# A chunked attention and its MLP on one core: the order written out by hand, attention of the next 384 tokens between the steps of the MLP

## The chip, the cores and the metric

The kernel runs on one core of one Trainium2 chip. A core has five engines with a queue of instructions each: TensorE (PE, with its weight loads shown apart as PEld) multiplies matrices and transposes, VectorE (DVE), ScalarE (ACT) and GpSimd (POOL) work on tiles, and SyncE (SP) issues transfers. Matrix products land in PSUM, an accumulator memory of eight banks; everything else lies in SBUF. Transfers from and to memory are issued from POOL's or SP's queue and run on 16 DMA engines. The metric is the time on the device in microseconds (us), lower is better.

## What is computed

Two stages in a row, over 4 batches of 768 tokens. Inputs and output are float32.

```python
def _attn_ref(q, k, v, mem_k, mem_v):          # q, k, v: (4, 8, 768, 64); mem: 8 rows per head
    chunk, left_ctx, right_ctx = (32, 16, 8)
    for c in range(nc):                        # 24 chunks of 32 tokens
        l_start = max(0, c_start - left_ctx)
        r_end = min(S, c_end + right_ctx)
        k_full = np.concatenate([mem_k, k[:, :, l_start:r_end]], axis=2)
        v_full = np.concatenate([mem_v, v[:, :, l_start:r_end]], axis=2)
        scores = scale * np.matmul(q_c, k_full.transpose(0, 1, 3, 2))
        a = np.exp(scores - max)
        out[:, :, c_start:c_end] = np.matmul(a / sum(a), v_full)

def _moe_ref(x, g_ln, w_ch1, w_ch2):           # x: (4, 768, 512), the heads side by side
    xn = (x - mu) / np.sqrt(var + 1e-06) * g_ln
    return x + np.maximum(xn @ w_ch1, 0.0) @ w_ch2      # 512 -> 2048 -> 512
```

Each chunk of 32 queries sees at most 56 keys around it and 8 memory keys. The second stage is a layer normalisation and an MLP with a residual.

## The kernel before

The kernel works batch by batch and has seven segments, each a function. All matrices are held in float16, cast by the transfers that load them.

`load_kq` and `load_v` (issued from POOL, L98, L102, L111, L116, L120) bring k, q and v of a batch; tokens stand on the partitions in blocks of 128, so a transfer consists of rows of 64 elements. `v16` holds, for each of eight groups of 96 queries, the 120 value rows around it (neighbouring groups overlap) behind 8 memory rows that `bcast_mem_v` copies (L130), and a column of ones that gives the sum of the softmax.

`seg_B(b)` transposes k and q with TensorE, head by head (L188, L193 for the memory keys, L210), into a PSUM tile `trp` of 64 partitions; DVE copies k into `slabs` in four pieces (L198, L199, L203, L204), so that each group of 96 queries has its own 128 keys beside the memory keys, and q into `QT` (L215).

`seg_C(b)` computes, for each group and half of the heads, four products of 128 keys by 96 queries (L222), and ACT takes the exponential in three pieces with a bias `bandcol` that puts keys outside a chunk's band at -50 (L231).

`seg_D(b)` multiplies the weights with the values (L253) in blocks of 32, 64 or 96 rows, divides by the sum (L261, L264), and normalises: statistics on DVE (L270, L271), the square root on ACT (L272), reciprocal and shift on DVE (L276, L277), and the application on ACT (L282).

`seg_E(b)` transposes the normalised rows (L292) and ACT copies them out (L297). `seg_F(b, pi)` is the up projection of 384 tokens: 16 PSUM tiles of 128 x 384, four matmuls each (L305), and the ReLU on DVE (L311). `seg_G(b, pi)` is the down projection: three PSUM tiles of 128 x 512, sixteen matmuls each (L320), the residual on DVE (L327) and the store from SP (L328).

PSUM is shared as four banks `trp`, two `mm` (scores, values and the up projection take turns there) and two `f2p`. The code asks for the segments in the order F, C, G, F, D, G, B, E for each batch (L341 to L354), but the order in which each engine gets its instructions is set by a scheduler that may move any instruction forward past others that do not depend on it. In the trace, for example, the scores of the next batch run between down matmuls, and single down matmuls between up groups.

The weights come by `load_w1` and `load_w2` (L134, L141); `scale_w1` multiplies the layer norm's gain into `w1s` (L178). In the order of POOL's queue they stand behind k, q and v of the first batches.

## Time and profile before

| | us |
|---|---|
| median of 3 runs | 315.42 |
| lowest and highest run | 315.36, 317.46 |
| profiled execution, span from the first to the last instruction | 317.2 |

| engine | busy us in the profiled execution |
|---|---|
| PE | 275.5 |
| PEld | 158.7 |
| DVE | 183.2 |
| ACT | 102.0 |
| POOL | 71.9 |

A busy time adds up the stretches in which an engine has at least one instruction under way. Matmuls overlap each other, so a busy TensorE need not be a TensorE at its peak: the distance from one start to the next says how dense it is. The chain of waits follows the last instruction back to what released each step. A group of instructions is given with its line, its engine, output and inputs by the program's names, shapes, count, busy time and the mean duration of one; behind the bar stands how long the engine had been idle before them and what ended that. In a timeline, instructions of one kind that follow one another are merged, with their count.

### The profile page before, as it was taken

Reading aid. Unit: us, or ns where it says so; the run is one execution under the profiler, and the core shown is the slowest. Engines: PE = TensorE matmul, PEld = TensorE weight load, DVE = VectorE, ACT = ScalarE, POOL = GpSimd, SP = SyncE. Lnnn points to the kernel's source line nnn. Section 1 sums busy time; section 2 is a strip of 40 time slices with the busy share of each in tenths; the row PEclk is TensorE's granted clock in tenths of the full one; section 3 lists DMA queues with packets and bytes.
Section 4 is the critical chain, followed back from the end, with each engine's and each line's share of the span. In section 5 each row is a group of like instructions: output and inputs, shape, how many; then the busy total and the mean of one; then the engine's idle time right before and its main releaser. Section 6 shows DMA issues by size and latency. Waiting matters only on the chain.

```text
span 317.2 us, 5313 instructions
## 1 busy us (share of the span) xinstructions
PE 275.5 (87%) x2112; PEld 158.7 (50%) x2112; DVE 183.2 (58%) x519; ACT 102.0 (32%) x264; POOL 71.9 (23%) x88
## 2 busy tenths in 40 slices
PE   0794776497999999799999999789999995999994
PEld 0673655363534555475434554655435543455441
DVE  3571369953614787956506788957117784577411
ACT  0026734330287014330494034230990145100000
POOL 8977052993000020900000012800000000000000
PEclk9999999997999999969999999799999999799999
DMA  8999999999991021950011031910010010000121
GB/s 51 155 124 140 194 151 144 86 130 200 160 87 68 1 18 66 108 36 2 0 67 36 0 51 39 127 10 2 33 36 33 2 66 35 0 0 2 55 77 66
DMA packets 90695, 21.11 MB, mean 67 GB/s; under 512 B 85040, under 2 KB 87088, under 8 KB 90672
## 3 DMA queue, kind: packets, MB, share of 16 engines
q0 software_dynamic: 86688, 14.50, 63.0%
q1 hardware_dynamic: 3984, 6.30, 5.4%
q8 instruction: 16, 0.26, 0.4%
q14 instruction: 7, 0.06, 0.1%
HBM read 28.97 MB, written 6.29 MB: 111 GB/s over the span
## 4 chain that ended last, share of the span: by engine, by line
PE 76%; DVE 8%; DMA 5%; ACT 5%; POOL 3%; issue 2%; ACTq 0%; POOLq 0%; DVEq 0%
PE f2p L320 28%; PE mm L305 26%; PE mm L222 6%; PE mm L253 5%; PE trp L210 5%; PE trp L188 4%; DMA w2s<-in_moe_w_ch_dram 3%; ACT AT L231 3%; DMA q<-in_q_dram 2%; DVE bnst L270 2%; ACT xnT L297 1%; DVE x L264 1%; DVE w1s L178 1%; POOL v L111 1%; PE trp L193 1%
## 5 line engine op out<-in xcount | busy, mean ns | idle before, releaser
L320 PE MATMUL f2p<-w2s,reluT 128*128 128x512 f16 x384 | 106.5, 382 | 2.2 <-DMA w2s<-in_moe_w_ch_dram 2.2
L305 PE MATMUL mm<-xnT,w1s 128*128 128x384 f16 x512 | 99.4, 332 | 3.8 <-ACT xnT L297 2.7
L311 DVE TENSOR_SCALAR reluT<-mm 128x384 f16<-128x384 f32 x128 | 71.0, 557 | 46.1 <-PE mm L305 41.1
L305 PEld LDWEIGHTS <-w1s 128*128 128x128 f16 x512 | 49.8, 99 | 44.5 <-issue 11.1
L231 ACT ACTIVATE AT<-mm,bandcol 128x128 f16<-128x128 f32 x192 | 53.9, 369 | 9.0 <-PE mm L222 6.7
L320 PEld LDWEIGHTS <-reluT 128*128 128x128 f16 x384 | 31.2, 97 | 28.7 <-issue 0.2
L327 DVE TENSOR_TENSOR out_sb<-f2p,x 128x512 f32<-128x512 f32 x24 | 16.5, 686 | 45.0 <-PE f2p L320 45.0
L188 PE MATMUL trp<-identity,k 128*64 128x128 f16 x192 | 25.9, 282 | 17.7 <-DMA k<-in_k_dram 9.1
L111 POOL DMA_DIRECT2D v<-in_v_dram x32 | 27.5, 866 | 28.2 <-PE mm L253 26.4
L116 POOL DMA_DIRECT2D v<-in_v_dram x8 | 6.6, 819 | 103.6 <-PE mm L253 103.5
L188 PEld LDWEIGHTS <-k 128*64 128x64 f16 x192 | 18.7, 147 | 22.3 <-issue 12.1
L253 PEld LDWEIGHTS <-AT 128*64 128x64 f16 (+2 forms) x448 | 20.1, 115 | 19.4 <-issue 14.8
L253 PE MATMUL mm<-v,AT 128*64 128x65 f16 (+2 forms) x448 | 25.4, 212 | 4.9 <-DVE x L264 4.9
L222 PE MATMUL mm<-QT,slab 64*128 64x96 f16 x256 | 24.1, 221 | 5.6 <-ACT AT L231 5.6
L222 PEld LDWEIGHTS <-slab 64*128 64x128 f16 x256 | 14.5, 102 | 27.8 <-issue 27.8
L282 ACT ACTIVATE xn<-x,negmr,rstd 128x512 f16<-128x512 f32 x24 | 19.5, 813 | 23.7 <-DVE negmr L277 23.7
L231 ACT ACT_TABLE_LOAD x4 | 5.1, 1283 | 60.3 <-DVE reluT L311 39.8
L210 PE MATMUL trp<-identity,q 128*64 128x128 f16 x192 | 23.8, 280 | 0.7 <-DMA q<-in_q_dram 0.7
L199 DVE COPY slab<-trp 64x720 f16<-64x720 f16 x32 | 16.4, 514 | 8.8 <-PE mm L222 8.7
L272 ACT ACT_TABLE_LOAD x4 | 5.1, 1283 | 47.5 <-DVE recip L261 47.4
L264 DVE TENSOR_TENSOR x<-mm,recip 128x256 f32<-128x256 f32 x48 | 19.7, 411 | 0.4
L215 DVE COPY QT<-trp 64x768 f16<-64x768 f16 x32 | 17.2, 538 | 2.0 <-PE trp L210 1.8
(36 smaller groups left out, 166.0 us busy)
## 6 DMA issues: line engine op xcount, KB each, us to landing
out_dram<-out_sb SPq DMA_DIRECT2D x24, 256.0 KB, 2.0
k<-in_k_dram POOLq DMA_DIRECT2D x8, 384.0 KB, 8.4
q<-in_q_dram POOLq DMA_DIRECT2D x8, 384.0 KB, 8.9
v<-in_v_dram POOLq DMA_DIRECT2D x32, 90.0 KB, 4.7
w1s<-in_moe_w_ch_dram POOLq DMA_DIRECT2D x4, 512.0 KB, 13.7
w2s<-in_moe_w_ch_dram POOLq DMA_DIRECT2D x4, 512.0 KB, 11.9
v<-in_v_dram POOLq DMA_DIRECT2D x16, 60.0 KB, 4.2
mem_k<-in_mem_k_dram POOLq DMA_DIRECT2D x1, 32.0 KB, 2.8
```

Of the source, the lines that this page charges most:

```text
L111: nc.gpsimd.dma_start(out=v16[hh][8:128, hp, 1:7, 0:64], in_=dram_ap(v, base + hp * S * D + 80 * 64, [[64, 120], [96 * 64, 6], [1, 64]]),)
L188: nc.tensor.matmul(out=ktr[:, 128 * i : 128 * i + 128], lhsT=k16[b % 2][:, h, i, :], rhs=identity, is_transpose=True, start=(i == 0), stop ...
L210: nc.tensor.matmul(out=qtr[:, 128 * i : 128 * i + 128], lhsT=q16[b % 2][:, h, i, :], rhs=identity, is_transpose=True, start=(i == 0), stop ...
L215: nc.vector.tensor_copy(out=QT[hh][:, hp, :], in_=qtr)
L222: nc.tensor.matmul(out=sc[:, QG * hp : QG * hp + QG], lhsT=slabs[4 * hh + hp][:, g, :], rhs=QT[hh][:, hp, QG * g : QG * g + QG], start=(hp ...
L231: nc.scalar.activation(out=atv[:, :, 32 * t : 32 * t + 32], in_=scv[:, :, 32 * t : 32 * t + 32], func=mybir.ActivationFunctionType.Exp, bi ...
L253: nc.tensor.matmul(out=av[r0:r1, hp, :], lhsT=ATt[g][hh][:, QG * hp + ql : QG * hp + ql + (r1 - r0)], rhs=v16[hh][:, hp, g, :], start=(hp ...
L264: nc.vector.tensor_tensor(out=xs[t][b % 2][:, 256 * hh : 256 * hh + 256], in0=av[:, :, 0:64], in1=rc_b, op=mybir.AluOpType.mult,)
L282: nc.scalar.activation(out=xn16[t], in_=xt, func=mybir.ActivationFunctionType.Identity, bias=negmr[j], scale=rstd[j],)
L305: nc.tensor.matmul(out=o, lhsT=w1s[dt][:, 128 * hc : 128 * hc + 128], rhs=xnT[dt][:, 384 * pi : 384 * pi + 384], start=(dt == 0), stop=(dt ...
L311: nc.vector.tensor_scalar(out=reluT[pi][hc], in0=o, scalar1=0.0, scalar2=None, op0=mybir.AluOpType.max,)
L320: nc.tensor.matmul(out=o2, lhsT=reluT[pi][hc][:, 128 * (t % 3) : 128 * (t % 3) + 128], rhs=w2s[hc // 4][:, hc % 4, :], start=(hc == 0), st ...
```

## The change

The kernel is written anew around units of 384 tokens, and the scheduler is switched off: each engine runs its instructions in the order in which the code asks for them. While the MLP of unit u runs, the attention of unit u+1 is put between its steps.

A unit has 28 steps: 16 up steps (four matmuls of 384 columns and a ReLU) and 12 down steps (four matmuls of 512 columns, the residual and the store after each fourth). The attention of 128 tokens is a call of `scores`, one of `values` and one of `turn_x`; three of each follow steps 1, 5, 10, then 8, 12, 17, then 15, 19, 24. In units 0, 2 and 4 the next batch's keys and queries are transposed by four calls of `kq_block` after steps 3, 7, 11 and 17. The loads of a batch to come stand at step 20 of units 0 and 2 (`load_kq`) and at steps 2 to 5 of units 1 and 3 (`load_v` and what belongs to it).

Shapes change as well:

- k and q lie with 8 tokens of a head on a partition (96 partitions), so a transfer has rows of 512 elements. `kq_block` transposes two heads of k and q, 32 transposes of 96 columns, to the two halves of 128 partitions. DVE copies k and ACT copies q out, each as 768 elements on 128 partitions. `KT` holds the keys in blocks of 72 columns, 64 tokens and 8 memory keys, so that a group of 64 queries finds all its keys in 104 neighbouring rows and no keys are copied twice.
- `scores` takes groups of 64 queries: eight matmuls of 64 columns and 64 rows per group, alternating between the two row halves and between two PSUM banks, and two exponentials of 256 elements on 104 partitions, with the band as a bias.
- `values`: sixteen matmuls of 65 columns, alternating between the two groups, whose outputs lie on the two halves of the partitions. The division is one instruction of 512 elements instead of two of 256.
- The normalisation: statistics on DVE as before; the shift, the sum with 1e-6, its power of -1/2 and the application to the row (512 elements) are four instructions on POOL. ACT has no part in it.
- The ReLU goes to ACT in odd up steps and stays on DVE in even ones.
- The value rows of neighbouring groups are copied on the chip (`load_v_halo`, `load_v_mem`, from SP) instead of being loaded twice.
- The weights lie in chunks by output column, `w1c`, `w2c`, and are loaded, in the order of POOL's queue, w1 behind k and q of batch 0 and the first 7 of its 12 value blocks, then the other 5 blocks, then w2, and k, q and v of batch 1 behind all of these.
- PSUM: `att` has two tiles of two banks each, `f1p` two of one bank (up), `f2p` two of one bank (down).

The core of the diff, the new code:

```diff
+    ctx.enter_context(tc.manual_schedule())
+    att = [ps.tile([128, 2, 512], FP32, name=f"att{i}") for i in range(2)]
+    f1p = [ps.tile([128, 384], FP32, name=f"f1p{i}") for i in range(2)]
+    f2p = [ps.tile([128, 512], FP32, name=f"f2p{i}") for i in range(2)]
...
+    def load_kq(b):
+        for dst, src in ((k16, k), (q16, q)):
+            nc.gpsimd.dma_start(
+                out=dst[b % 2][:, :, :, :],
+                in_=dram(src, b * H * HS, [[512, 96], [HS, H], [1, 512]]),
+            )
+    def load_v(b, g0, g1):
+        vt = V[b % 2]
+        for g in range(g0, g1):
+            nc.gpsimd.dma_start(
+                out=vt[24:88, g, :, 0:64],
+                in_=dram(v, b * H * HS + 64 * g * D, [[64, 64], [HS, H], [1, 64]]),
+            )
...
+    def mem_cols(b):
+        src = memKT[:, 4 * b : 4 * b + 4, :]
+        nc.gpsimd.tensor_copy(
+            out=free(KT[b % 2], 16, [[KC, 4], [BLK, NG + 1], [1, 8]]),
...
+    def kq_block(b, j):
+        p = slot("att")
+        for half, src in ((0, k16), (1, q16)):
+            pv = as16(p[:, half, :])
+            for r in range(8):
+                for par in range(2):
+                    nc.tensor.matmul(
+                        out=pv[64 * par : 64 * par + 64, 96 * r : 96 * r + 96],
+                        lhsT=src[b % 2][:, 2 * j + par, r, :], rhs=identity[0:96, 0:96],
+                        is_transpose=True, start=True, stop=True,
+                        tile_position=(0, 64 * par),
+                    )
+        pk, pq = as16(p[:, 0, :]), as16(p[:, 1, :])
+        nc.vector.tensor_copy(
+            out=free(KT[b % 2], j * KC + 24, [[BLK, NG], [8, 8], [1, 8]]),
+            in_=free(pk, 0, [[8, NG], [1, 8], [96, 8]]),
+        )
+        nc.scalar.copy(
+            out=free(QT[b % 2], j * S, [[8, 96], [1, 8]]),
+            in_=free(pq, 0, [[1, 96], [96, 8]]),
+        )
+    def scores(b, t):
+        for g in (2 * t, 2 * t + 1):
+            p = slot("att")
+            a = AT[g % 4]
+            for j in range(4):
+                for par in range(2):
+                    nc.tensor.matmul(
+                        out=p[:, par, 64 * j : 64 * j + 64],
+                        lhsT=KT[b % 2][64 * par : 64 * par + 64, j, BLK * g : BLK * g + 128],
+                        rhs=QT[b % 2][64 * par : 64 * par + 64, j, 64 * g : 64 * g + 64],
+                        start=(j == 0), stop=(j == 3), tile_position=(64 * par, 0),
+                    )
+            for c in range(2):
+                nc.scalar.activation(
+                    out=free(a, 32 * c, [[64, 2], [128, 4], [1, 32]], KR),
+                    in_=free(p, 32 * c, [[512, 2], [64, 4], [1, 32]], KR),
+                    func=ACTF.Exp, bias=band[0:KR, cls, c : c + 1], scale=0.125,
+                )
+    def values(b, t, x):
...
+        for h in range(H):
+            for gg in range(2):
+                nc.tensor.matmul(
+                    out=p[64 * gg : 64 * gg + 64, h // 4, c0 : c0 + HD],
+                    lhsT=AT[g % 4][0:KR, h, :], rhs=V[b % 2][0:KR, g, h, :],
+                    start=(h % 4 == 0), stop=(h % 4 == 3), tile_position=(0, 64 * gg),
+                )
...
+        nc.vector.bn_stats(out=bst[i], in_=x)
+        nc.vector.bn_aggr(out=mv[i], in_=bst[i])
+        nc.gpsimd.tensor_scalar(out=lnc[i][:, 0:1], in0=mv[i][:, 0:1], scalar1=-1.0, scalar2=1.0, op0=ALU.mult, op1=ALU.mult)
+        nc.gpsimd.tensor_scalar(out=lnc[i][:, 1:2], in0=mv[i][:, 1:2], scalar1=1e-6, scalar2=1.0, op0=ALU.add, op1=ALU.mult)
+        nc.gpsimd.tensor_tensor(out=lnc[i][:, 2:3], in0=lnc[i][:, 1:2], in1=mhalf[:, 0:1], op=ALU.pow)
+        nc.gpsimd.tensor_scalar(
+            out=xn[i], in0=x, scalar1=lnc[i][:, 0:1], scalar2=lnc[i][:, 2:3],
+            op0=ALU.add, op1=ALU.mult,
+        )
...
+        if hc % 2:
+            nc.scalar.activation(out=rT[u % 2][hc], in_=p, func=ACTF.Relu)
+        else:
+            nc.vector.tensor_scalar(
+                out=rT[u % 2][hc], in0=p, scalar1=0.0, scalar2=None, op0=ALU.max
+            )
...
+    nc.gpsimd.dma_start(out=memk16, in_=dram(mem_k, 0, [[64, 8], [512, B * H], [1, 64]]))
+    load_kq(0)
+    nc.gpsimd.dma_start(out=memv16[:, :, :, 0:64], in_=dram(mem_v, 0, [[64, 8], [512, B * H], [1, 64]]))
+    load_v(0, 0, 7)
+    make_identity(nc, identity)
+    load_w1(0)
...
+    mem_keys()
+    mem_cols(0)
+    load_w1(1)
+    load_w1(2)
+    load_w1(3)
+    load_v(0, 7, NG)
+    for c in range(4):
+        load_w2(c)
+    mem_cols(1)
...
+    for j in range(4):
+        kq_block(0, j)
+    scores(0, 0)
+    scores(0, 1)
+    values(0, 0, xs[0])
+    scores(0, 2)
+    values(0, 1, xs[1])
+    turn_x(0, 0)
+    values(0, 2, xs[2])
+    turn_x(0, 1)
+    for c in range(4):
+        scale_w1(c)
+    turn_x(0, 2)
+    load_kq(1)
+    load_v_halo(0, 6, NG)
+    load_v(1, 0, NG)
...
+    for u in range(NU):
+        b1, half = (u + 1) // 2, (u + 1) % 2
...
+        if u + 1 < NU:
+            for i in range(3):
+                t = 3 * half + i
+                at(1 + 7 * i, scores, b1, t)
+                at(5 + 7 * i, values, b1, t, xs[(3 * (u + 1) + i) % 9])
+                at(10 + 7 * i, turn_x, u + 1, i)
+        if u % 2 == 0 and u // 2 + 1 < B:
+            bn = u // 2 + 1
+            for j in range(4):
+                at((3, 7, 11, 17)[j], kq_block, bn, j)
+            if bn + 1 < B:
+                at(20, load_kq, bn + 1)
+        if u % 2 == 1 and u // 2 + 2 < B:
+            bn = u // 2 + 2
+            at(2, load_v, bn, 0, NG)
+            at(3, mem_cols, bn)
...
+        for step in range(28):
+            if step < 16:
+                up(u, step)
+            else:
+                down(u, (step - 16) // 4, (step - 16) % 4)
+            for fn, args in plan.get(step, ()):
+                fn(*args)
```

More of the change, by code (lines that the diff above doesn't have):

```diff
@@ L45 @@
     identity = sb.tile([128, 128], FP16, name="identity")
[L46 to L47 removed]
+    memk16 = sb.tile([8, B * H, 64], FP16, name="memk16")
+    memv16 = sb.tile([8, B, H, HD], FP16, name="memv16")
+    memKT = sb.tile([128, B * 4, 8], FP16, name="memKT")
     g_col = sb.tile([128, 4], FP32, name="g_col")
[L49 to L50 removed]
@@ new lines, in as16 @@
+    def as16(t):
+        return t.bitcast(FP16)
+    HS = S * D
+    def load_kq(b):
[11 more added lines that the diff above has]
+            )
```

472 lines of the change are left out of this document (180 added, 292 removed).

## The prediction

> **What bounds the kernel now.** I read the page first (span, busy time, chain), then busy time by stretches, then TensorE's timeline.
>
> ```profile
> span 317.2 us, 5313 instructions
> PE 275.5 (87%) x2112; PEld 158.7 (50%) x2112; DVE 183.2 (58%) x519; ACT 102.0 (32%) x264; POOL 71.9 (23%) x88
> GB/s 51 155 124 140 194 151 144 86 130 200 160 87 68 1 18 66 108 36 2 0 67 36 0 51 39 127 10 2 33 36 33 2 66 35 0 0 2 55 77 66
> PE 76%; DVE 8%; DMA 5%; ACT 5%; POOL 3%; issue 2%; ACTq 0%; POOLq 0%; DVEq 0%
> HBM read 28.97 MB, written 6.29 MB: 111 GB/s over the span
> q0 software_dynamic: 86688, 14.50, 63.0%
> ```
>
> By stretches (columns: stretch, busy time and instructions of each engine, granted TensorE clock, DMA share, GB/s written):
>
> ```profile
> core 0: us, PE busy (x) PEld busy (x) DVE busy (x) ACT busy (x) POOL busy (x), PEclk, DMA share, GB/s
> 9.00:25.00 16.00, 14.78 (x114) 11.71 (x115) 11.06 (x41) 2.53 (x6) 14.19 (x24) 1.00 2.77 134
> 25.00:42.00 17.00, 11.63 (x102) 9.04 (x102) 2.93 (x11) 13.47 (x46) 4.87 (x7) 1.00 1.85 181
> 143.00:212.00 69.00, 65.57 (x527) 36.19 (x527) 45.00 (x130) 25.47 (x66) 10.24 (x12) 0.98 0.30 38
> ```
>
> TensorE ends the chain, but 87% is an average of two unlike parts. From 143 to 212 us, one batch of the steady loop, TensorE is idle for 3.4 us; from 25 to 42 us it is idle for 5.4 while the loads run at their highest. How dense the loop is shows only in start-to-start distances, in TensorE's timeline (start, length, operation):
>
> ```profile
> 74.54 0.38 PE L320 MATMUL f2p<-w2s,reluT 128*128 128x512 f16 x1 [2.22 <-DMA w2s<-in_moe_w_ch_dram]
> 74.75 2.21 PE L305 MATMUL mm<-xnT,w1s 128*128 128x384 f16 x8
> 76.76 0.63 PE L320 MATMUL f2p<-w2s,reluT 128*128 128x512 f16 x1
> 77.19 2.22 PE L305 MATMUL mm<-xnT,w1s 128*128 128x384 f16 x8
> 79.25 0.38 PE L320 MATMUL f2p<-w2s,reluT 128*128 128x512 f16 x1
> ...
> 86.43 0.34 PE L222 MATMUL mm<-QT,slab 64*128 64x96 f16 x4
> 86.70 1.90 PE L320 MATMUL f2p<-w2s,reluT 128*128 128x512 f16 x8
> 88.54 0.34 PE L222 MATMUL mm<-QT,slab 64*128 64x96 f16 x4
> ...
> 106.67 1.46 PE L305 MATMUL mm<-xnT,w1s 128*128 128x384 f16 x8
> 107.97 0.38 PE L320 MATMUL f2p<-w2s,reluT 128*128 128x512 f16 x1
> ...
> 116.78 0.33 PE L253 MATMUL mm<-v,AT 128*64 128x65 f16 x8
> 117.04 1.04 PE L320 MATMUL f2p<-w2s,reluT 128*128 128x512 f16 x4
> ...
> 128.85 0.52 PE L210 MATMUL trp<-identity,q 128*64 128x128 f16 x6
> 129.21 0.50 PE L188 MATMUL trp<-identity,k 128*64 128x128 f16 x6
> ```
>
> and, from the chain of waits, its last stretch of TensorE and a group of exponentials:
>
> ```profile
> 36.59 1.67 ACT AT L231 x6
> ...
> 295.37 17.71 PE f2p L320 x82
> ```
>
> Eight 384-column matmuls take 106.67 to 107.97: 0.1625 us each. The last 82 of 512 columns take 17.71: 0.216. The MLP is 512 x 0.1625 + 384 x 0.216 = 166.1 us before and after. A 128-column transpose in a warm stream takes (129.21 - 128.85)/6 = 0.06 us, a 65-column value matmul (117.04 - 116.78)/8 = 0.0325, the shortest spacing here. Eight down matmuls between score groups take 88.54 - 86.70 = 1.84 instead of 1.73, and the four scores 0.27 instead of 4 x 0.0425 (96 columns at the 384-column rate): about 0.1 on entry, 0.1 on exit, 0.2 per excursion.
>
> So of 317.2 us, 166 are MLP matmuls, some 70 are a start that waits for loads (at 74.54 the first down matmul still waits for `w2s`), 4.1 are the tail (313.08 to the end), and the rest is attention inside three loop rounds of 69 us.
>
> **The change, part by part.** Other prices, from the groups (last numbers: busy time, mean ns of one, idle before), then three rows of the timeline:
>
> ```profile
> L231 ACT ACTIVATE AT<-mm,bandcol 128x128 f16<-128x128 f32 x192 | 53.9, 369 | 9.0 <-PE mm L222 6.7
> L297 ACT ACTIVATE xnT<-trp 128x768 f16<-128x768 f16 x16 | 12.0, 810 | 18.1 <-PE trp L292 13.2 <-DVE slab L204 4.8
> L311 DVE TENSOR_SCALAR reluT<-mm 128x384 f16<-128x384 f32 x128 | 71.0, 557 | 46.1 <-PE mm L305 41.1
> L327 DVE TENSOR_TENSOR out_sb<-f2p,x 128x512 f32<-128x512 f32 x24 | 16.5, 686 | 45.0 <-PE f2p L320 45.0
> L270 DVE BATCH_NORM_STATS2 bnst<-x 128x6 f32<-128x512 f32 x24 | 16.4, 683 | 0.0
> L261 DVE RECIPROCAL recip<-mm 128x4 f32<-128x4 f32 x48 | 8.1, 169 | 7.7 <-PE mm L253 7.4
> L215 DVE COPY QT<-trp 64x768 f16<-64x768 f16 x32 | 17.2, 538 | 2.0 <-PE trp L210 1.8
> L155 POOL TENSOR_SCALAR_AFFINE_SELECT bandcol<-zcol 128x3 f32<-128x3 f32 x2 | 0.4, 194 | 0.0
> masks.py:199 POOL TENSOR_SCALAR_AFFINE_SELECT identity<-identity 128x128 f16<-128x128 f16 x1 | 0.3, 304 | 0.1
> L120 POOL DMA_DIRECT2D v<-in_v_dram x8 | 6.3, 790 | 0.0
> ```
>
> ```profile
> 3.22 1.44 POOL L98 DMA_DIRECT2D k<-in_k_dram  x1
> 9.07 0.85 PE L188 MATMUL trp<-identity,k 128*64 128x128 f16 x6 [9.07 <-DMA k<-in_k_dram]
> 17.87 2.50 POOL L111 DMA_DIRECT2D v<-in_v_dram  x3 [1.78 <-DMA q<-in_q_dram]
> ```
>
> *TensorE in the loop.* A unit is 384 tokens: 16 up steps of 4 x 0.1625 = 0.65 and 12 down steps of 4 x 0.216 = 0.866, 20.8 us. Beside it stand, three times, scores (16 matmuls), values (16) and `turn_x` (4 transposes, 0.23). Values: 16 x 0.0325 + 0.2 = 0.72. Scores have 64 columns and load 128-column weights; no row shows a pair on two row halves, so their spacing lies between 0.0145 (two at once at the 64-column rate of 0.029) and 0.0425 (the 96-column one); I take 0.0325, the nearest measured small matmul: 0.72. `kq_block`: 32 transposes of 96 columns, alternating between column halves: between 0.021 (pairs at once) and 0.0425 (one by one); I take the middle, 0.032, so 1.22 with the excursion. A unit with the next one's attention is 20.8 + 3 x (0.72 + 0.72 + 0.23) = 25.8; units 0, 2 and 4 carry four `kq_block`s more: 30.7; unit 7 is 20.8.
>
> *DVE and ACT.* The page's busy times (183 and 102) would not bind, but the order is now fixed, and `f1p` has two buffers: up step n waits for the ReLU of step n-2. After values(5) DVE does reciprocal 0.17, multiply 0.69, statistics 0.68, aggregate 0.17 = 1.71, and only then ReLU 6 (0.557). By hand, from a unit's start: values end at 5.42, DVE's chain at 7.26, ReLU 6 at 7.82; TensorE is ready for up 8 at 6.72 and starts at 7.85: 1.1 lost. After scores(8), four exponentials of 256 elements hold ACT: 0.369 + 128 x 0.69 ns (the slope from the 768-element copy, 0.81) = 0.46 alone; six of 128 take 1.67, 0.28 apart, 0.09 less than one lasts, so four take some 1.5; ReLU 9 follows and up 11 waits 0.2. Elsewhere results are early. An odd unit is 27.2 us. In an even one the `kq_block` at step 7 covers the 1.1; with its own copies (768 scattered elements on DVE, between 0.54 as the packed `QT` copy and 0.94 at the 1 ns per element between L311 and L327; I take 0.94) I find 0.3: 31.0. Bounds: no stall to 3 us per unit.
>
> *Normalisation moves from ACT to POOL*: three one-column instructions (about 0.2 each, as the 3-element select) and one over 512 elements: 0.19 + 0.45 by the slope between the two selects, up to 0.9 for its two operations; 1.5 together. In an odd unit DVE's chains end at 7.3, 14.8 and 21.95, and TensorE comes to `turn_x` at 10.5, 17.4 and 24.4: 3.2, 2.6 and 2.45 us. Covered, so nothing; if the cover goes, each microsecond is paid per tile. ACT's switches between exponential and square root go too, none on TensorE's path.
>
> *POOL's queue.* The tile scheduler before hid the load issues; now `load_v` (12 issues of 0.8) stands before the unit's normalisation. At 17.87 the fourteenth POOL transfer waits for the sixth, the second `q`: eight are in flight at most. In unit 0 (31.0 long) values(19) end at 23.9, DVE at 25.8, POOL at 27.3; it then issues `load_kq(2)`, six `v`, and stops until k and q (3.15 MB) have landed, then five more issues and `mem_cols`. q lands at 27.3 + 3 (before bytes flow) + 3.15/0.362 = 39.0; five issues (4.0), `mem_cols` (0.7, as a select) and the normalisation (1.5) make 45.2, which is 14.2 of unit 1, whose `turn_x` is due at 10.5: 3.7 lost, and likewise in unit 3: 7 us (0 to 10).
>
> *The start.* Loads run at 181 GB/s written between 25 and 42 us; q0 writes 14.5 MB for 28.97 read, so 362 GB/s read. Until `kq_block(1, 0)` at step 3 of unit 0 the queue carries kq(0) 3.15, v(0) 1.57, w1 and w2 8.39, kq(1) 3.15 = 16.25 MB, one behind the other; before, v(1) and kq(2) also stood ahead of w2. The first 0.79 MB landed 5.8 us after its issue (3.22 to 9.07), 3.6 more than its bytes; with `k` issued at 2.2 by a shorter instruction the flow starts at 5.2, 16.25/0.362 = 44.9 later it is 50, and I add 3 for gaps: the identity now stands behind seven `v` issues and thus behind q's landing (about 14), the weights behind it and behind twelve selects. q(1) lands at 53 (bounds: 46 at 400 GB/s, twice the 200 of the page's fastest slice, 66 at the 268 that 134 written in 9:25 gives). The MLP itself can start earlier: from an identity at 15.5, 128 transposes of 0.05 to 0.1 and three tiles of scores, values and normalisation (some 5 each) end at 38 to 44. TensorE then reaches step 3 and waits, so the landing decides.
>
> *The sum*, in the profiled execution's time: landing 53; rest of unit 0 from the q half of that block, 31.0 - 3.9 = 27.1; TensorE's slow first steps after a wait, 1.5 (the eight after 74.75 and the eight after 77.19 take 2.0 each for 1.3); units 1, 3, 5, 6: 4 x 27.2 = 108.8; units 2 and 4: 62.0; unit 7: 20.8; POOL 7; tail 4.1: 284.3. That profile, 317.2, lies 1.8 above the median of 315.42, so 282.5.
>
> **A rule against a row.** The row: values at 0.0325 us run one column block after another, so this trace cannot show two blocks at once. The Trainium skill, "TensorEngine Tiling (Array Packing)", section Tiling Modes, says tiles operate independently and can run weight loads and matmuls in parallel. By it the pairs of this change overlap, and the sum would be that of the first rival, 271, for 282.5 by the row; no run here shows it.
>
> **The rivals.**
> 1. *Pairs run side by side.* Spacing halves to 0.021 in `kq_block` and 0.0145 in scores: in the loop 11 x 32 x 0.011 + 21 x 16 x 0.018 = 3.9 + 6.0, and values at half of 0.0325 another 5.5, of which DVE's waits in odd units take back some 4: 271. For it: even units have few waits. Against: none of today's spacings is below 0.03.
> 2. *The fixed order stalls more.* Each unit loses 3 us more, since any late ReLU holds all behind it: 7 x 3 = 21, 303. For it: DVE's 1.7 us chains stand before ReLUs and f1p has two buffers. Against: down steps need no fresh ReLU.
> 3. *Slower than before: POOL normalises too slowly.* Mean cover 2.8 us. Beyond it every microsecond costs 21 us in the loop and 3 at the start; from 282.5 to 1% above 315.4 takes 36, so POOL would need 4.3 us per tile where I count 1.5; at 4.5, about 323. For it: no row has POOL arithmetic on 512 columns. Against: 128 elements take 0.304. The Trainium skill, "GPSIMD Engine Reference", section Performance versus the Vector engine, speaks against such work there: some 2.6 cycles per element at 1.2 GHz, as an estimate 1.1 us for 512 elements; the group would then take 1.9, still covered.
> 4. *Not what it says:* start and order change, but the gain is eaten by slower loads (66 for 53) and rival 2 together: 316, no change.
>
> **How the numbers follow.** Forecast 0.42, rival 1 0.25, rival 2 0.20, rival 3 0.05, rival 4 0.05, other 0.03. The forecast's own bounds are 264 (landing 46, no POOL or ReLU waits) to 300 (landing 66, POOL 10). The range 264 to 306 takes in rivals 1 and 2. One per cent is about what a measurement of this kernel can tell: faster 0.90, within 0.05, slower 0.05.
>
> **What would show it.** Right: the first up step starts before 45 us and the first down step near 68; TensorE's longest wait is for `q` or `k` near 45 to 55; rounds of two units last 58 to 62 us instead of 69; up steps wait 1 us for a ReLU; one `turn_x` of units 1 and 3 waits for POOL. Wrong: POOL's 512-column instruction far above 1 us, `turn_x` waiting in every tile, up waits of several microseconds per unit, or weights landing after 60.

## The result and the profile after

The changed kernel takes 303.98 us (median of 4 runs, 303.54 to 305.10), the kernel before 315.49 beside it (315.36 to 317.46). The ratio is 0.964, with a 95% interval of 0.959 to 0.969: faster by 3.6%, where 10.4% was forecast. A mechanism that the forecast priced at 7 us cost more than three times as much. The profiled execution of the kernel before was a slow one: its span of 317.2 us lies above all its spans beside the experiments, 311.2 to 316.6.

The page of the changed kernel: its span, the busy times and the chain by engine.

```profile
span 301.9 us, 5523 instructions
PE 226.7 (75%) x2288; PEld 122.4 (41%) x2288; DVE 124.1 (41%) x253; ACT 79.6 (26%) x177; POOL 92.4 (31%) x185
PE 57%; DMA 17%; POOL 8%; DVE 8%; issue 5%; ACT 2%; DVEq 0%; POOLq 0%; ACTq 0%
```

TensorE's busy time fell from 275.5 to 226.7 us, the span only from 317.2 to 301.9. In the chain TensorE's share went from 76% to 57%, that of transfers from 5% to 17% and that of POOL from 3% to 8%. So the kernel has less work on its path and more waits. The stretches say where (stretch, busy time and instructions of each engine, granted TensorE clock, DMA share, GB/s written). They are units 1, 2, 3 and 5, cut within 0.04 us of the start of each unit's first up step:

```profile
core 0: us, PE busy (x) PEld busy (x) DVE busy (x) ACT busy (x) POOL busy (x), PEclk, DMA share, GB/s
87.50:126.40 38.90, 26.42 (x222) 13.32 (x221) 12.67 (x26) 8.20 (x20) 12.38 (x24) 0.87 1.41 93
126.40:155.91 29.51, 28.45 (x350) 15.69 (x348) 16.13 (x30) 11.20 (x24) 7.99 (x16) 1.00 0.11 31
155.91:193.53 37.62, 27.17 (x221) 13.75 (x220) 12.88 (x26) 8.20 (x20) 12.37 (x24) 0.86 1.28 96
223.10:249.50 26.40, 24.90 (x222) 12.87 (x221) 12.58 (x26) 8.20 (x20) 5.12 (x12) 1.00 0.08 31
```

Units 1, 3 and 5 do the same work on TensorE, DVE and ACT (the same counts, except for one record that is missing). Unit 5 takes 26.40, units 1 and 3 take 38.90 and 37.62. What these two have more is POOL work (24 instructions instead of 12) and transfers (93 and 96 GB/s instead of 31). TensorE's timeline (start, length, operation, and in brackets the idle time before it and what ended it) gives the start and the place in units 1 and 3:

```profile
38.54 0.61 PE L250 MATMUL att<-identity,xn 128*128 128x128 f16 x4 [6.99 <-POOL xn L241]
...
47.72 2.72 PE L264 MATMUL f1p<-xT,w1c 128*128 128x384 f16 x8 [2.79 <-DVE xT L255]
...
54.97 0.53 PE L171 MATMUL att<-identity,k 96*64 96x96 f16 x16 [2.67 <-DMA k<-in_k_dram]
59.27 0.85 PE L171 MATMUL att<-identity,q 96*64 96x96 f16 x16 [3.77 <-DMA q<-in_q_dram]
...
88.89 0.41 PE L194 MATMUL att<-QT,KT 64*128 64x64 f16 x16
89.23 2.96 PE L264 MATMUL f1p<-xT,w1c 128*128 128x384 f16 x16
...
95.12 0.81 PE L264 MATMUL f1p<-xT,w1c 128*128 128x384 f16 x4 [1.15 <-DVE rT L273]
...
96.21 1.47 PE L264 MATMUL f1p<-xT,w1c 128*128 128x384 f16 x8
109.02 0.60 PE L250 MATMUL att<-identity,xn 128*128 128x128 f16 x4 [11.34 <-POOL xn L241]
109.41 2.77 PE L264 MATMUL f1p<-xT,w1c 128*128 128x384 f16 x8
...
175.39 0.61 PE L250 MATMUL att<-identity,xn 128*128 128x128 f16 x4 [9.30 <-POOL xn L241]
...
275.86 11.67 PE L264 MATMUL f1p<-xT,w1c 128*128 128x384 f16 x64
```

The first `turn_x` of units 1 and 3 waits 11.34 and 9.30 us for POOL's normalised rows, and the eight matmuls behind the first wait take 2.77 us instead of 1.47. POOL's own timeline shows what stood ahead of that normalisation:

```profile
84.56 0.85 POOL L95 DMA_DIRECT2D k<-in_k_dram  x1
85.41 0.78 POOL L95 DMA_DIRECT2D q<-in_q_dram  x1
86.17 4.04 POOL L103 DMA_DIRECT2D V<-in_v_dram  x6
95.21 0.68 POOL L103 DMA_DIRECT2D V<-in_v_dram  x1 [5.01 <-DMA k<-in_k_dram]
101.06 0.67 POOL L103 DMA_DIRECT2D V<-in_v_dram  x1 [5.17 <-issue]
...
106.48 0.54 POOL L158 COPY KT<-memKT 128x416 f16<-128x416 f16 x1
106.99 0.20 POOL L230 TENSOR_SCALAR lnc<-mv 128x1 f32<-128x1 f32 x1
...
108.19 0.77 POOL L241 TENSOR_SCALAR xn<-xs,lnc 128x512 f16<-128x512 f32 x1
```

POOL issues k, q and six value blocks of batch 2 one behind the other: eight transfers. The ninth issue waits until k has landed, the tenth until q has landed, the others follow about 1 us apart, each when another transfer is done. For the tenth and the later ones the profile names no releaser here (in unit 3 it names q for the tenth), but the landings in the trace do: q at 100.5 us, the value blocks behind it at 101.5, 102.6 and 103.6, and each of these issues starts some 0.55 us later. The normalisation of unit 1 had its input long before; it stands behind these waits in POOL's queue.

### The profile page after: what moved, and what is told of

It is laid out like the page before. It is cut to its first block, busy times and chain, and to the rows that moved or that the text cites. A ratio compares the mean times of both kernels' runs of the same rounds, so it can differ in the third digit from the quotient of the medians.

```text
span 301.9 us, 5523 instructions
## 1 busy us (share of the span) xinstructions
PE 226.7 (75%) x2288; PEld 122.4 (41%) x2288; DVE 124.1 (41%) x253; ACT 79.6 (26%) x177; POOL 92.4 (31%) x185
## 4 chain that ended last, share of the span: by engine, by line
PE 57%; DMA 17%; POOL 8%; DVE 8%; issue 5%; ACT 2%; DVEq 0%; POOLq 0%; ACTq 0%
PE f2p L284 26%; PE f1p L264 23%; DMA q<-in_q_dram 13%; DMA w1c<-in_moe_w_ch_dram 4%; PE att L213 3%; PE att L171 2%; PE att L250 2%; PE att L194 2%; DVE bst L228 2%; DVE xs L221 2%; POOL V L103 2%; DVE KT L178 2%; POOL xn L241 1%; ACT QT L182 1%; POOL lnc L238 1%
## 5 line engine op out<-in xcount | busy, mean ns | idle before, releaser
L264 PE MATMUL f1p<-xT,w1c 128*128 128x384 f16 x512 | 101.4, 341 | 8.9 <-DVE rT L273 5.3
L284 PE MATMUL f2p<-w2c,rT 128*128 128x512 f16 x384 | 87.8, 379 | 0.0
L271 ACT ACTIVATE rT<-f1p 128x384 f16<-128x384 f32 x64 | 31.7, 496 | 151.8 <-PE f1p L264 151.7
L264 PEld LDWEIGHTS <-w1c 128*128 128x128 f16 x512 | 48.9, 101 | 46.0 <-issue 18.9
L273 DVE TENSOR_SCALAR rT<-f1p 128x384 f16<-128x384 f32 x64 | 35.2, 550 | 41.6 <-PE f1p L264 41.5
L284 PEld LDWEIGHTS <-rT 128*128 128x128 f16 x384 | 35.7, 98 | 39.5
L103 POOL DMA_DIRECT2D V<-in_v_dram x48 | 32.3, 685 | 37.8 <-DMA q<-in_q_dram 13.9
L201 ACT ACTIVATE AT<-att,band 104x256 f16<-104x256 f32 x96 | 37.6, 480 | 9.5 <-PE att L194 9.5
L250 PE MATMUL att<-identity,xn 128*128 128x128 f16 x96 | 10.5, 239 | 31.7 <-POOL xn L241 31.6
L241 POOL TENSOR_SCALAR xn<-xs,lnc 128x512 f16<-128x512 f32 x24 | 18.9, 786 | 2.6
L228 DVE BATCH_NORM_STATS2 bst<-xs 128x6 f32<-128x512 f32 x24 | 16.7, 694 | 0.8
L194 PEld LDWEIGHTS <-KT 64*128 64x128 f16 x384 | 8.1, 98 | 13.5 <-issue 13.1
L213 PEld LDWEIGHTS <-AT 104*64 104x64 f16 x384 | 9.0, 120 | 10.5 <-issue 8.5
```

The source lines that it names most:

```text
L103: nc.gpsimd.dma_start(out=vt[24:88, g, :, 0:64], in_=dram(v, b * H * HS + 64 * g * D, [[64, 64], [HS, H], [1, 64]]),)
L194: nc.tensor.matmul(out=p[:, par, 64 * j : 64 * j + 64], lhsT=KT[b % 2][64 * par : 64 * par + 64, j, BLK * g : BLK * g + 128], rhs=QT[b % 2 ...
L201: nc.scalar.activation(out=free(a, 32 * c, [[64, 2], [128, 4], [1, 32]], KR), in_=free(p, 32 * c, [[512, 2], [64, 4], [1, 32]], KR), func= ...
L228: nc.vector.bn_stats(out=bst[i], in_=x)
L241: nc.gpsimd.tensor_scalar(out=xn[i], in0=x, scalar1=lnc[i][:, 0:1], scalar2=lnc[i][:, 2:3], op0=ALU.add, op1=ALU.mult,)
L250: nc.tensor.matmul(out=pv[:, 128 * dt : 128 * dt + 128], lhsT=xn[i][:, 128 * dt : 128 * dt + 128], rhs=identity, is_transpose=True, start= ...
```

## The experiments

All kernels were timed beside the kernel before on the same chip; ratios are against it, with 95% intervals. The medians of these comparisons for the kernel before lie between 314.5 and 315.7.

### Values behind the last normalisation

```diff
-            at(2, load_v, bn, 0, NG)
-            at(3, mem_cols, bn)
-            at(4, load_v_mem, bn)
-            at(5, load_v_halo, bn, 0, NG)
+            at(20, load_v, bn, 0, NG)
+            at(21, mem_cols, bn)
+            at(22, load_v_mem, bn)
+            at(23, load_v_halo, bn, 0, NG)
```

> The value loads of batches 2 and 3 (twelve issues on POOL, with mem_cols and the copies on the chip) move from steps 2 to 5 of units 1 and 3 to steps 20 to 23, behind the last normalisation of the unit. Theory (POOL's queue: the issues are held until k and q of the next batch have landed, and the normalisation stands behind them): the two waits of turn_x, 11.3 and 9.3 us, and the slow matmuls after them go; units 1 and 3 take 26.5 us as unit 5 does, instead of 38.9 and 37.6; some 23 us less, about 281. Rival (the transfers themselves cost the time, wherever they stand, through DVE, POOL or TensorE slowed by traffic): the loss moves into units 2 and 4, which grow by about 10 us each; about 302.

Measured: 282.05 us (279.36 to 284.47), ratio 0.893 (0.886 to 0.901), 21.9 us less than the changed kernel. In TensorE's timeline the first `turn_x` of unit 1 no longer waits, and the next unit's first up step comes 26.4 us after 88.47:

```profile
88.47 1.46 PE L264 MATMUL f1p<-xT,w1c 128*128 128x384 f16 x8
...
98.49 0.39 PE L250 MATMUL att<-identity,xn 128*128 128x128 f16 x4
...
114.88 1.30 PE L264 MATMUL f1p<-xT,w1c 128*128 128x384 f16 x7
```

The same bytes are loaded, at another place in POOL's queue, and unit 2, where they now run, is not longer (29.53 us, before 29.55). So the loss of units 1 and 3 was the order in POOL's queue and not the transfers as such.

The transfers do take part in it. Between 84 and 112 us, in the view of transfers (issues, KB each, us to landing), q of batch 2 took this long in the changed kernel

```profile
q<-in_q_dram POOLq DMA_DIRECT2D x1, 768.0 KB, 15.1
```

and this long with the value blocks out of the way:

```profile
q<-in_q_dram POOLq DMA_DIRECT2D x1, 768.0 KB, 13.1
```

### k and q behind the value blocks

```diff
-            if bn + 1 < B:
-                at(20, load_kq, bn + 1)
...
             at(2, load_v, bn, 0, NG)
+            at(2, load_kq, bn)
```

> load_kq of batches 2 and 3 moves from step 20 of units 0 and 2 to directly behind load_v at step 2 of units 1 and 3; load_v stays ahead of the normalisation. If what holds the value issues is the landing of k and q ahead of them: the wait of turn_x falls from 11.3 and 9.3 to under 2 us, about 283 to 285. If the twelve value issues and their transfers of 1 us each are enough by themselves: 5 us or more of each wait stay, about 293 or more.

Measured: 282.66 us (281.13 to 284.27), ratio 0.898 (0.892 to 0.905). POOL's timeline and TensorE's:

```profile
98.58 0.77 POOL L95 DMA_DIRECT2D q<-in_q_dram  x1 [1.17 <-DMA V<-in_v_dram]
```

```profile
101.89 0.40 PE L250 MATMUL att<-identity,xn 128*128 128x128 f16 x4 [2.10 <-POOL xn L241]
102.13 1.46 PE L264 MATMUL f1p<-xT,w1c 128*128 128x384 f16 x8
```

All fourteen issues still stand ahead of the normalisation, and yet the wait is 2.10 us instead of 11.34, and in unit 3 none reaches 1 us. What POOL waits for is now a value block of 64 KB, at most 1.2 us at a time, not the landing of q's 768 KB. The number of issues was the smaller part; the landing that they waited for was the larger. The eight matmuls behind the wait of 2.10 us take 1.46, so they are not slow.

### Six value blocks only

```diff
-            at(2, load_v, bn, 0, NG)
+            at(2, load_v, bn, 0, 6)
             at(3, mem_cols, bn)
             at(4, load_v_mem, bn)
-            at(5, load_v_halo, bn, 0, NG)
+            at(20, load_v, bn, 6, NG)
+            at(21, load_v_halo, bn, 0, NG)
```

> As the changed kernel, but at step 2 of units 1 and 3 only the first six value blocks are loaded; the other six follow at step 20 of the same unit. With k and q of the next batch ahead of them that makes eight transfers under way. Theory (no more than eight transfers of POOL's queue are under way, the ninth waits for the first): none of the six waits for k or q, POOL is free for the normalisation some 6 us after the k issue, the waits of turn_x (11.3 and 9.3 us) vanish, about 280 to 283. Rival (value loads behind k and q hold POOL whatever their number, in proportion): about half of the wait stays, 4 us or more in each of the two units, about 292.

Measured: 281.25 us (279.31 to 282.12), ratio 0.893 (0.888 to 0.899). POOL's timeline:

```profile
88.44 3.99 POOL L103 DMA_DIRECT2D V<-in_v_dram  x6
92.43 0.54 POOL L158 COPY KT<-memKT 128x416 f16<-128x416 f16 x1
```

With k, q and six blocks in flight POOL goes straight on to `mem_cols`, and `turn_x` waits in neither unit. Half of the blocks left in place cost nothing, so the cost is not proportional to them: it begins with the ninth transfer.

### Pairs one half after the other

```diff
-            for r in range(8):
-                for par in range(2):
+            for par in range(2):
+                for r in range(8):
                     nc.tensor.matmul(
```

This is the order of the transposes in `kq_block`: eight on one column half, then eight on the other.

> In kq_block the sixteen transposes of a tile no longer alternate between the two column halves: eight go to the lower half, then eight to the upper. If the alternation makes pairs run side by side (16 transposes start within 0.365 us now, 0.023 each): they take 16 x 0.0425 = 0.68, eleven blocks in the loop cost 0.6 us more each where nothing else holds TensorE, 3 to 7 us more in all. If the order of the halves does not matter: no change, 302 to 304.

Measured: 306.18 us (306.07 to 306.29), ratio 0.973 (0.965 to 0.980). In TensorE's timeline the 32 transposes of a block, alternating, as in the changed kernel:

```profile
129.49 0.53 PE L171 MATMUL att<-identity,k 96*64 96x96 f16 x16
129.86 0.51 PE L171 MATMUL att<-identity,q 96*64 96x96 f16 x16
```

and half after half (the first and the last row of such a block; between them stand three of q and three of k, alternating, where the two overlap):

```profile
130.08 0.60 PE L171 MATMUL att<-identity,k 96*64 96x96 f16 x13
...
130.63 0.58 PE L171 MATMUL att<-identity,q 96*64 96x96 f16 x13
```

Alternating, sixteen take 129.86 - 129.49 = 0.37, 0.023 each. In turn the whole block ends 130.63 + 0.58 - 130.08 = 1.13 after its start instead of 0.88, and in the middle k's second half still overlaps q's first. By the start times, the two transposes of an alternating pair start 0.003 us apart and the next pair 0.04 later; on one half they follow each other at 0.043. Alternating halves therefore do run side by side. That is the first rival of the prediction, and its price is small, less than the 0.6 us per block that was expected: 12 blocks in the loop x 0.25 = 3.0 us. The medians differ by 2.2, less than their intervals can tell apart, but the stretches show it: units 2 and 4, with four blocks each, take 30.46 and 30.47 us instead of 29.55 and 29.53, and units 5 and 6, which have none, take 26.4 as before.

### The last unit's ReLUs

```diff
-        if hc % 2:
+        if hc % 2 or u == NU - 1:
             nc.scalar.activation(out=rT[u % 2][hc], in_=p, func=ACTF.Relu)
```

> In the last unit, where nothing stands between the up steps, all sixteen ReLUs go to ACT (0.50 us each) instead of eight to DVE (0.55). If the two buffers of f1p and the ReLU's latency make an up step 0.72 us where its matmuls take 0.65: the 64 up matmuls take 10.6 to 11.0 instead of 11.5 us. If TensorE's own spacing is 0.18 there: 11.5 as before.

One run: 304.22 us, of which only this unit is read. The 64 up matmuls of unit 7 take 11.02 us from the first start to the first down matmul, 276.87 to 287.89, where the changed kernel takes 11.51 (275.86 to 287.37). That is 0.69 per up step instead of 0.72, where the prediction had 0.65. A shorter ReLU shortens the step. The start times show the rest: matmuls follow each other at 0.162 us, the 0.1625 of the prediction, and only every eighth distance is longer, 0.324 in the changed kernel and 0.255 here. In the changed kernel ReLU 0 of this unit ends at 277.27 and up 2 starts at 277.32. So the two `f1p` buffers and the ReLU behind them, not TensorE's rate, make the step longer.

### The start: k and q of batch 1 ahead of the down weights

```diff
+    load_kq(1)
     for c in range(4):
         load_w2(c)
...
     turn_x(0, 2)
-    load_kq(1)
```

> load_kq(1) is issued ahead of the four w2 loads instead of behind them and behind the first normalisations. Theory (the landing of q(1) at 59.3 decides when unit 0 goes on after step 3): the waits for k and q between 52 and 59 go, w2 lands before the first down step needs it, 6 to 8 us less, about 296 to 298. Rival (the sum of all loads decides): TensorE waits for w2 at the first down step instead, no more than 2 us less.

Measured: 302.55 us (300.50 to 305.51), ratio 0.959 (0.952 to 0.966): no difference to the changed kernel that can be told, and a miss. TensorE's waits for k and q are gone; in their place stand

```profile
41.76 0.61 PE L250 MATMUL att<-identity,xn 128*128 128x128 f16 x4 [9.82 <-POOL xn L241]
...
68.37 0.40 PE L250 MATMUL att<-identity,xn 128*128 128x128 f16 x4 [3.21 <-POOL xn L241]
```

and the reason stands in POOL's timeline:

```profile
36.14 3.09 POOL L132 DMA_DIRECT2D w2c<-in_moe_w_ch_dram  x4 [3.46 <-DMA w1c<-in_moe_w_ch_dram]
```

With k and q ahead of them, the four issues of w2 come only when more of w1 has landed, and the three first normalisations stand behind them: the wait of the first `turn_x` rises from 6.99 to 9.82. Part of that rise is spread: in the kernels of this study whose start is unchanged, the same wait lies between 6.99 and 8.71. The waits for k and q are gone and the time is not, so what held the start was not only the landing of q(1), as the prediction had it, but again POOL's order.

### The start: down weights behind the normalisations

The kernel with the values behind the last normalisation, and besides:

```diff
-    for c in range(4):
-        load_w2(c)
+    load_kq(1)
...
     turn_x(0, 2)
-    load_kq(1)
+    for c in range(4):
+        load_w2(c)
...
-    load_v(1, 0, NG)
-    load_v_halo(1, 0, NG)
...
+            if u == 0:
+                for j in range(3):
+                    at(6 + 7 * j, load_v, bn, 4 * j, 4 * j + 4)
+                at(21, load_v_halo, bn, 0, NG)
```

> On top of the first variant (value loads of batches 2 and 3 at step 20): load_kq(1) ahead of w2, w2 behind the three normalisations of the start, and the value loads of batch 1 in three parts behind the normalisations of unit 0. Theory (POOL's order decides the start too: the early normalisations wait for the w2 issues, unit 0 for q(1)): the waits for k and q at step 3 go, the first turn_x comes some 3 us earlier, 8 to 11 us less than the first variant, 271 to 274. Rival (the bytes decide): TensorE waits for w2 at the first down step, less than 4 us gained.

Measured: 277.92 us (276.85 to 278.36), ratio 0.883 (0.878 to 0.888), 4.1 less than with the values moved alone, where more was expected. TensorE's timeline:

```profile
35.01 0.61 PE L250 MATMUL att<-identity,xn 128*128 128x128 f16 x4 [3.42 <-POOL xn L241]
...
89.20 0.65 PE L213 MATMUL att<-V,AT 104*64 104x65 f16 x16 [6.68 <-issue]
89.78 4.05 PE L264 MATMUL f1p<-xT,w1c 128*128 128x384 f16 x12
```

The first up step starts at 44.32 instead of 47.72 and unit 0 ends at 77.83 instead of 87.50. Then the first value matmuls of unit 1 wait 6.68, with slow matmuls behind: 12 in 4.05, where the same twelve take 2.21 elsewhere in this trace. The profile names no releaser ("issue"). SP's queue gives a candidate: the halo copies, which the values need, were issued at

```profile
80.82 0.56 SPq L112 DMA_DIRECT2D V<-V  x1
```

because they cover all groups and so waited for the last value block, though unit 1 reads groups 0 to 5 alone.

### An earlier start

```diff
-    load_v(0, 0, 7)
     make_identity(nc, identity)
+    load_v(0, 0, 7)
...
-    turn_x(0, 0)
+    scale_w1(0)
     values(0, 2, xs[2])
+    turn_x(0, 0)
+    scale_w1(1)
     turn_x(0, 1)
-    for c in range(4):
-        scale_w1(c)
     turn_x(0, 2)
+    scale_w1(2)
+    scale_w1(3)
```

> The last variant, and in the start: the identity ahead of the value loads on POOL, all three value tiles on TensorE before the first turn_x, and the scaling of w1 spread between them on DVE instead of all sixteen ahead of the last copy. Expected: the first up step near 40 us instead of 47.7, unless the value halo or the weights hold it; 5 to 8 us less than the variant before, 264 to 268.

Measured: 279.90 us (279.09 to 281.11), ratio 0.890 (0.885 to 0.895): a miss by some 12 us. The first up step starts at 40.32, 4.0 earlier, as expected; but unit 0 then waits 4.72 for q at 50.78, ends at 78.86, and the halo wait of unit 1 is 7.26:

```profile
50.78 0.85 PE L171 MATMUL att<-identity,q 96*64 96x96 f16 x16 [4.72 <-DMA q<-in_q_dram]
...
90.81 0.65 PE L213 MATMUL att<-V,AT 104*64 104x65 f16 x16 [7.26 <-issue]
```

An earlier start that runs into the next landing gains nothing.

### The halo in parts

The kernel with the down weights behind the normalisations, and:

```diff
-                at(21, load_v_halo, bn, 0, NG)
+                at(13, load_v_halo, bn, 0, 3)
+                at(20, load_v_halo, bn, 3, 7)
+                at(24, load_v_halo, bn, 7, NG)
```

> The kernel with the weights' second half behind the three normalisations, and the copies between the value blocks of batch 1 (SP) cut into three calls: groups 0 to 2 at step 13 of unit 0, 3 to 6 at step 20, the rest at step 24. Theory (the 6.68 us that the first value matmuls of unit 1 waited is the halo, which SP could issue only when the last value block had landed, at 80.8, and not the rate of the matmuls): the values of unit 1 need the blocks and copies of groups 0 to 5 alone, whose copies then land by about 80, so the wait goes and with it the half-speed matmuls behind it (about 1.6): 277.9 - 6.7 - 1.6 = 269 to 271. Rival (the copies are slow because k, q of batch 2 and the value blocks share the engines of the DMA; in parts they land no earlier): the wait stays at 4 us or more, 275 to 278.

Measured: 269.58 us (268.21 to 270.82), ratio 0.856 (0.851 to 0.862), 8.3 less, as expected. In TensorE's timeline the value matmuls of unit 1 now follow the up matmuls without a wait:

```profile
77.81 2.96 PE L264 MATMUL f1p<-xT,w1c 128*128 128x384 f16 x16
80.70 0.45 PE L213 MATMUL att<-V,AT 104*64 104x65 f16 x16
```

The cause that the profile could not name is thereby shown: copies that asked for more than their reader needs.

### The early start with the halo in parts

The early start with the same three calls, and in unit 0 the blocks of k and q later:

```diff
-                at((3, 7, 11, 17)[j], kq_block, bn, j)
+                at(((12, 16, 20, 23) if u == 0 else (3, 7, 11, 17))[j], kq_block, bn, j)
```

> The early start (first up step at 40.3) with the same three calls of copies, and in unit 0 the four blocks of k and q at steps 12, 16, 20 and 23 instead of 3, 7, 11 and 17, behind the landing of q at 50.8. Theory (what the early start gained was given back in two waits, 4.72 for q in unit 0 and 7.26 for the copies in unit 1, each with slow matmuls behind it): both go, 279.9 - 4.7 - 1.3 - 7.3 - 1.6 = 265, range 263 to 267. Rival (the rest of unit 0 is held by the second half of the weights, which land while it runs): one wait for w2c or for a value block takes the place of that for q, 268 to 273.

Measured: 266.69 us (265.96 to 267.50), ratio 0.848 (0.842 to 0.854), as expected. The early start, which gave nothing before, is worth 2.9 us here, together with the later blocks of k and q. The wait for q in unit 0 is gone; up 15 now waits 2.10 for ReLU 13, which in ACT's order stands behind the copy of q.

### ReLU 6 on ACT

```diff
-        if hc % 2:
+        if hc % 2 or u == NU - 1 or (hc == 6 and (u % 2 or u in (0, 6))):
```

> The early start with the copies in parts, and the ReLU of up step 6 on ACT instead of DVE in units 0, 1, 3, 5 and 6, and all ReLUs of unit 7 on ACT. Theory (the 1.15 us that up 8 waits in these units is DVE's chain of four instructions ahead of ReLU 6, as the prediction has it, and ACT is free at that time): the wait goes in all five, ACT's two ReLUs 6 and 7 in a row cost 0.1 to 0.3 at up 9, and unit 7 gives 0.5: 266.7 - 5 x 0.95 - 0.5 = 261 to 262. Rival (the wait only moves: ReLU 7 behind ReLU 6 on ACT holds up 9, then the exponentials of step 8 come late): each unit gains under 0.4, 264 to 266.

Measured: 261.19 us (259.83 to 262.19), ratio 0.827 (0.821 to 0.832), as expected, and the fastest kernel of this study: 17.3% less than before, 14% less than the changed kernel. In TensorE's timeline ups 6 to 8 run through in unit 1,

```profile
80.33 2.21 PE L264 MATMUL f1p<-xT,w1c 128*128 128x384 f16 x12
```

where the changed kernel waited 1.15. A unit of this kind takes 25.2 us (75.33 to 100.49) instead of 26.4. Unit 0 gives 1.2 back, 34.75 us instead of 33.51: behind the wait for ReLU 13, which the kernel without this edit has too, the granted clock is 0.50 from 59.8 to 63.1, and four down matmuls take 1.89 instead of 1.04.

```profile
58.68 0.81 PE L264 MATMUL f1p<-xT,w1c 128*128 128x384 f16 x4 [2.09 <-ACT rT L271]
...
59.77 1.89 PE L284 MATMUL f2p<-w2c,rT 128*128 128x512 f16 x4
```

## Why the prediction was wrong

The direction was right, the size was not. Its sum beside the trace of the changed kernel, cut at the same places:

| term | predicted | measured | difference |
|---|---|---|---|
| q of batch 1 has landed | 53 | 59.3 | +6.3 |
| rest of unit 0, with slow first steps (27.1 + 1.5) | 28.6 | 28.2 | -0.4 |
| units 1 and 3 without POOL's term | 54.4 | 52.8 (as units 5 and 6) | -1.6 |
| POOL's term in units 1 and 3 | 7 | 23.7 (76.5 - 52.8) | +16.7 |
| units 2 and 4 | 62.0 | 59.1 | -2.9 |
| units 5 and 6 | 54.4 | 52.8 | -1.6 |
| unit 7 and tail | 24.9 | 26.0 | +1.1 |
| span | 284.3 | 301.9 | +17.6 |

**POOL's queue: the step that failed, by its size.** The prediction named this mechanism, both units and the instruction that would wait, and priced it at 3.7 us per unit; it cost 11.34 and 9.30 of waiting and with the slow matmuls 23.7 in both. In unit 1 the difference of 7.6 has four parts:

- POOL was free only 2.9 us before the unit began (84.56 to 87.50), for 3.7: 0.8.
- q had landed and POOL went on 16.5 after its first issue (84.56 to 101.06), for 11.7: 4.8. The prediction divided the bytes of k and q by the start's best rate and put nothing for the six value blocks in flight beside them. Without these q lands 2.0 earlier (13.1 for 15.1 after its issue); for the other 2.8 a rate lower than assumed is the likely cause, which no run tests.
- From q's landing to the normalised rows passed 7.9 (101.06 to 108.96), for 6.2: 1.7. The prediction counted the held issues at their own length, 0.8; but each waits for another transfer to land, and they came about 1 us apart. The normalisation takes 1.97 instead of 1.5.
- `turn_x` was due 10.2 after the unit's start, for 10.5: 0.3.

The forecast then left out what a wait of this length brings: TensorE at half speed for some 1.3 us behind it. The prediction counted that for the start but not here. Its upper bound for both units, 10, lies below the wait of one. Two parts worked on each other (value blocks slow q, q's landing releases value blocks), and all four errors had the same sign.

**The start.** The landing came 6.3 later: 16.25 MB from 5.2 to 59.3 are 300 GB/s read on the average, for the 362 of the best stretch of before. The signs around it came late too: first up at 47.72 (before 45 was forecast) and first down at 75.03 (near 68); the longest of the waits for k and q there is 3.77, and TensorE's longest wait is not for them but for POOL. But the landing alone did not decide the start: with k and q earlier nothing was gained. Putting POOL's order, the landing and the halo right together moved the kernel from 282.05 to 266.69, 15.4 us.

**TensorE in the loop.** Here the first rival was right: pairs on two halves run side by side. By the start times the two matmuls of a pair start 0.003 us apart and the next pair follows 0.03 later, so sixteen scores start within 0.22 us, 0.014 each on the average, for the 0.0325 assumed. What is left of the 89.23 - 88.89 = 0.34 is the way out, 0.12 from the last score to the next up matmul, beside some 0.1 on the way in: the 0.2 per excursion was right. The rival was right in its mechanism, not in its total, since a second error went the other way. An up step takes 0.72, not 0.65, in unit 7, which has nothing else to wait for: the prediction counted results as early there, and the ReLU is not. A call of scores or values costs 0.2 to 0.3 less than the prediction has it, together 1.6 us per unit, but units 5 and 6 are only 0.8 shorter than forecast. That the terms of the loop came near is thus in part luck, two errors against each other. "A rule against a row" weighed the Trainium skill, "TensorEngine Tiling (Array Packing)", section Tiling Modes, and took the row; the trace now agrees with the rule, by the 0.25 us that the other order costs per block.

**ReLU.** Up 8 of an odd unit waits 1.15, for the 1.1 worked out by hand from DVE's chain. Right, and shown by the last experiment. In even units it is 0.37 (0.3). The second rival, stalls everywhere, falls: the waits of up steps for DVE's ReLUs that the profile lists are 5.3 us in the whole trace, and the short ones of unit 7, 0.16 at every second step, add 1.1.

**Normalisation on POOL.** The prediction said that it is covered where POOL's queue is free. It is: `turn_x` waits for POOL five times in the whole trace, three times at the start (6.99, 0.74, 3.25) and once in each of units 1 and 3. The third rival falls with the group:

```profile
L241 POOL TENSOR_SCALAR xn<-xs,lnc 128x512 f16<-128x512 f32 x24 | 18.9, 786 | 2.6
L238 POOL TENSOR_TENSOR lnc<-lnc,mhalf 128x1 f32<-128x1 f32 x24 | 13.4, 558 | 2.0
```

The large instruction takes 0.79, below the 0.9 assumed. What made the group 1.97 is the power of a single column, 0.56, where 0.2 was assumed. (The 1.9 that the third rival gives for the group is a slip: 1.1 and three times 0.2 make 1.7.) The Trainium skill, "GPSIMD Engine Reference", section Elementwise — side-by-side cycle accounting, gives 768 to 769 ns for 512 elements in its best case; the trace agrees with that figure, and not with the two-input one that the prediction weighed.

**The conversion.** The prediction took the span to lie 1.8 above the median, as 317.2 does. But the time of the profiled run of the changed kernel is 303.64 for a span of 301.9: a span lies 1.7 below the time of its own run, and by that the profiled execution of before took about 319, longer than any of the runs shown. So 282.5 should have been 284.3 + 1.7 = 286. That is 3.5 of the miss of 21.5 us; 0.3 is the distance of the median from the profiled run, and 17.6 are the table's. A slip beside this: 96 columns at the 384-column rate are 0.0406 and 64 columns 0.0271, not the prediction's 0.0425 and 0.029; by it the sum moves by some 0.5 us.

## What to carry to other kernels

Where a hand-set order puts arithmetic and transfers into one queue, count the transfers in flight: as soon as the queue's limit is reached, every instruction behind the next issue waits for a landing, however small it is and however early its input was. Put issues behind the last arithmetic that another engine waits for, and let each transfer cover no more than what its next reader needs. When several waits stand in a row, removing one shows the next: price a change by the next thing that is late, and test by removing them together.

## What the hardware showed beside this

- A queue on POOL held with eight of its transfers in flight (at the start and in units 1 and 3 of the changed kernel); it went on some 0.5 us after one landed. Six blocks beside k and q cost nothing, twelve cost 11.3 us.
- Value blocks, rows of 64 elements, land about 1 us apart at 64 KB written each when they follow one another, some 65 GB/s, where the loads of the start ran at 181 before the change.
- Two matmuls on the two halves of the array started 0.003 us apart, and pairs followed at 0.03 (64 or 65 columns) to 0.04 (96 columns); on one half 96 columns followed at 0.043.
- After waits of 6.68 and 11.34 us TensorE ran at about half speed for the next matmuls (12 in 4.05 for 2.21, 8 in 2.77 for 1.47), after 1.15 us at full speed. In between the length of the wait did not decide: after 2.10 us the speed stayed in two kernels (k and q behind the value blocks, the early start with the halo in parts), but after the same wait of 2.09 us the fastest kernel ran at half the clock for 3.3 us, and the kernel before took 2.21 for eight matmuls after a wait of 2.22, for 1.46 elsewhere. The Trainium skill, "TensorE: Matmul & The Clock Gate", Part 1, says that an idle window of about 3.4 us halves the clock; the long waits agree with it, but by the length of the wait alone those of 2.09 and 2.22 do not.
